# The end of an attention and soft-MoE kernel: where the last raw values and weights lie, a merge in halves, and outputs of two or three tiles a transfer

## The chip, the cores and the metric

The kernel runs on one core of a Trainium2 chip. The metric is the device time of one execution in microseconds (us). The core has five engines that run by themselves and meet at semaphores: TensorE (PE, its weight loads PEld), VectorE (DVE), ScalarE (ACT), GpSimd (POOL) and SyncE (SP). Sixteen DMA engines move data between HBM and SBUF. TensorE writes into PSUM. DMAs that cast float32 to bfloat16 are issued from POOL here, the plain ones from SP.

## The reference

```python
batch, n_heads, seq, head_dim = (8, 12, 448, 64)
N, D, E, S_per_e, F = (3584, 768, 8, 4, 1024)
# attention with one extra exp(-m) in the denominator
scores = scale * np.matmul(q, k.transpose(0, 1, 3, 2))
m = np.max(scores, axis=-1, keepdims=True)
e = np.exp(scores - m)
attn = e / (np.sum(e, axis=-1, keepdims=True) + np.exp(-m) + 1e-09)
attn_out = np.matmul(attn, v)
x = attn_out.transpose(0, 2, 1, 3).reshape(B * S, H * D)
# soft mixture of experts over all 3584 rows, 32 slots, 4 of them to an expert
logits = x @ phi
d = np.exp(logits - logits.max(0, keepdims=True)); d /= d.sum(0, keepdims=True) + 1e-09
slot_input = (d.T @ x).reshape(E, S_per_e, D)
for e in range(E):
    slot_out[e] = np.maximum(slot_input[e] @ w1[e], 0.0) @ w2[e]
c = np.exp(logits - logits.max(1, keepdims=True)); c /= c.sum(1, keepdims=True) + 1e-09
return c @ slot_out.reshape(n_slots, D)
```

## The kernel before

The attention runs over U = 24 units; a unit `u` is two heads of two batches (`bp, hp = divmod(u, 6)`). The rows of a batch are numbered `(p t)`: P = 64 partitions by TB = 7 tiles. For each unit, `stage_T` transposes q and k on TensorE, `stage_S` makes scores for the row maxima, `stage_MT` turns these into a mask operand (`md`, made by POOL at lines 282 and 288), `stage_ST` makes the scores once more with the maxima subtracted, ACT takes the exponential (line 309), `stage_AV` multiplies with v, and `stage_N` divides by the denominator into `xbuf(u)`. `stage_V` (line 314) casts the raw v. The last unit leaves the detour through SBUF out: `stage_last` (lines 380 to 400) divides straight from PSUM, with `last_sinks` having prepared the denominators. `stage_X` transposes x for the logits; `mixture` keeps a running softmax over rows for the 32 slots and adds the weighted rows to `acc`; `slot_in` is the matmul of it.

All instructions are issued in an order written by hand: `at(n, where, f)` puts a piece of work into the plan at tick `n` (7 ticks a unit, `end` is 168), and one loop over ticks runs the pieces in the order small, scores, av, value, ST, rooms, value, end, load. An engine carries out its own instructions in this order.

SBUF is laid out by hand. `block` holds the attention's buffers (`parts`); when their last reader is done, the same places take expert weights: `rooms[0..7]`, each 3072 bfloat16 columns, four quarters of 768 (`j0`, `m` of `load_w`). Room 1 covers the end of the raw v (`vr`) and the raw q and k (`qr`, `kr`). The first 24 weight pieces lie in `wres`; pieces 24 to 31 (`WRES` + 0..7) are the second matrices of experts 4 to 7 and go to the rooms. The weight loads are issued from POOL, the v loads from SP. v of unit 23 is loaded into the places `qr` and `kr`, after the transposes of unit 23 have read them; `stage_V(23)` then frees three quarters of room 1.

After the attention, `merge` finds weights for four partial sums of the slots (`rden`, `fw`, `sums`), `slot_in` ends in PSUM, line 674 adds it to `acc` into `ld`, line 678 transposes and folds it by 12 matmuls, and `den` (line 671) with `rden` (lines 682 and 683) gives the denominators; line 685 writes the experts' input `SI`. `experts_hidden` (line 705) does the first expert layer. `outer` (line 824) does the second one, into two PSUM halves of 384 columns; its last piece, `(1,)` of `jh` 1, needs rooms 4 to 7. Its results go to `so`; `first_tiles` makes the first two output tiles, and a loop makes tiles 2 to 27 (matmul line 884, copy 888, output DMA 889). PSUM tiles come from `ring`, three places taken in turn by `slot`. Output tile `i` is kept at its own place in `wres` (`kept`), 3072 bytes a partition, and tiles `t` of one `bp` lie side by side both there and in the output.

Of the kernel before, what the change touches and what calls it, by code (L numbers as in the profile page):

```python
# [9 lines left out]
F32 = mybir.dt.float32  # L10
# [14 lines left out]
def kernel(  # L25
# [75 lines left out]
    def xbuf(u):  # L101
        return block[:, ds(xbuf_at((u + 4) % (HP + 1)), N2)]

    def xruns(u):

        runs = []
        for i in range(HP):
            at_ = (u + i + 4) % (HP + 1)
            if runs and at_ > 1 and i % 4:
                runs[-1][1] += 1  # L110
            else:
                runs.append([i, 1, xbuf_at(at_)])
        return [(i, k, block[:, ds(o, k * N2)].rearrange("p (i s n) -> p i s n", i=k, s=TB))
                for i, k, o in runs]
# [40 lines left out]
        RAW[0, "qr"] = t_  # L155

    def load_v(u):
        t_ = block[:, ds(parts["vr" if u < U - 1 else "qr"][0], 2 * N2)].bitcast(F32).rearrange("p (h n) -> p h n", h=2)
        RAW[u, "vr"] = load(u, t_, v, nc.sync if u else nc.gpsimd)

    W = {}
# [5 lines left out]
    def load_w(i, j0=0, m=None, p0=0, rows=128):  # L167


        kind, e, half = weights[i]  # L170
        if kind == 1:
            J, n = KC // 2, F
            src = moe_w1[e].rearrange("(p j) f -> p j f", p=128)[:, ds(half * J, J), :]
        else:
            J, n = FK // 2, DD
            src = moe_w2[e, ds(half * 128 * J, 128 * J)].rearrange("(p j) f -> p j f", p=128)
        js = ds(2 * j0, 2 * (m or J))
        t_ = room(i, n // 2)
        src = src.rearrange("p j (h n) -> p (j h) n", h=2)
        gdma(out=t_[ds(p0, rows), js, :], in_=src[ds(p0, rows), js, :])  # L180
        for j in range(j0, j0 + (m or J)):
            W[kind, e, half * J + j] = t_[:, ds(2 * j, 2), :]
# [187 lines left out]

    def last_sinks(u):
        em = EM.pop(u)
        ems = small.tile([128, 2, TB], F32, tag="den", name="den").rearrange("p b g -> p (b g)")
        DEN[u] = ems
        for b in range(2):
            nc.gpsimd.tensor_copy(
                ems[:, ts(b, 2 * C3)].rearrange("p (h c) -> p h c", h=2), em[:, :, ds(b * C3, C3)])
        nc.gpsimd.tensor_copy(ems[:, ds(4 * C3, 2)], em[:, :, TB - 1])

    def stage_last(u):  # L380
        av = AV.pop(u)
        ems = DEN.pop(u)
        drec = small.tile([128, 2, TB], F32, tag="rec", name="rec", bufs=1).rearrange("p b g -> p (b g)")
        x = xbuf(u).rearrange("p (s n) -> p s n", s=TB)
        main = av[:, :, ds(0, 2 * C3 * 65)].rearrange("p b (g e) -> p b g e", e=65)
        rest = av[:, :, ds(2 * C3 * 65, 65)]
        nc.vector.scalar_tensor_tensor(
            drec[:, ds(0, 4 * C3)].rearrange("p (b g) -> p b g", b=2), main[:, :, :, D], 1e-9,
            ems[:, ds(0, 4 * C3)].rearrange("p (b g) -> p b g", b=2), op0=ALU.add, op1=ALU.add)
        nc.vector.scalar_tensor_tensor(drec[:, ds(4 * C3, 2)], rest[:, :, D], 1e-9,  # L390
                                       ems[:, ds(4 * C3, 2)], op0=ALU.add, op1=ALU.add)
        nc.vector.reciprocal(drec, drec)
        for b in range(2):
            nc.vector.tensor_tensor(
                x[:, ds(b * C3, C3), :].rearrange("p c (h d) -> p h c d", h=2),
                main[:, b].rearrange("p (h c) e -> p h c e", h=2)[:, :, :, ds(0, D)],
                drec[:, ts(b, 2 * C3)].rearrange("p (h c) -> p h c", h=2).unsqueeze(3)
                    .broadcast_to([128, 2, C3, D]), op=ALU.mult)
        nc.vector.tensor_tensor(
            x[:, TB - 1, :].rearrange("p (h d) -> p h d", h=2), rest[:, :, ds(0, D)],  # L400
            drec[:, ds(4 * C3, 2)].unsqueeze(2).broadcast_to([128, 2, D]), op=ALU.mult)
        X[u] = x


# [27 lines left out]
    def mixture(bp, n, at):  # L432
# [78 lines left out]

        def slot_in():

            ps = slot([128, DD])
            for s, (i, k, x) in ([(s, r) for r in xruns(bp * HP) for s in range(TB)] if final else
                                 [(s, r) for s in range(TB) for r in xruns(bp * HP)]):
                    b, c = divmod(s, C3) if s < 2 * C3 else (0, C3)
                    cs = ds(32 * c, 32)
                    nc.tensor.matmul(ps[cs, ds(i * 128, k * 128)], d_sb[:, b, cs], x[:, :, s, :],
                                     start=(b == 0 and i % 4 == 0), stop=(b == 1 or c == C3),  # L520
                                     tile_position=(0, 32 * c), skip_group_check=True)
            for i in range(HP):
                X.pop(bp * HP + i)
            if first:
                nc.vector.tensor_copy(acc, ps)
            elif not final:
                rescale(acc, alpha, ps)
            else:
                last_state["ps"] = ps

        if final:
            at(n - 28, "end", lambda: logits((0, 1)))
# [10 lines left out]
            at(n, "load", lambda: nc.gpsimd.memset(SI, 0.0))  # L543
            at(n + 5, "small", slot_sum)
            at(n + 7, "end", slot_in)
            at(n + 7, "end", lambda: [load_w(WRES + i) for i in (6, 7)])
            at(n + 7, "end", lambda: gate_logits(1))
            at(n + 7, "end", lambda: last_state["gl"][1]())
            at(n + 7, "end", experts_in)
# [200 lines left out]
    for u in range(U):  # L750
# [64 lines left out]

    os_ = [slot([128, 384]) for half in range(2)]

    def outer(half, jh, gs):
        J = FK // 2
        for g in gs:  # L820
            for j in range(J):
                for e in range(4):
                    es = ds(32 * e, 32)
                    nc.tensor.matmul(os_[half][es, :], HT[jh][:, g, j, es],
# [14 lines left out]
        return out[ds(2 * bp * S, 2 * S), :].rearrange("(q t) d -> q t d", t=TB)[:, ds(t, n), :]  # L839

    def kept(i, n=1):
        return wres[:, 2 + i // 2, ds(i % 2 * 2 * DD, 2 * DD * n)].bitcast(F32)

    def first_tiles(half, copy):


        ps = slot([128, 2, 512])
        for i in range(2):
            nc.tensor.matmul(ps[:, i, ds(0, 384)], wide[:, ts(i, 128)], so[:, half, :],
                             start=True, stop=True)  # L850
        o = kept(0, 2).rearrange("p (i g n) -> p i g n", i=2, g=2)[:, :, half, :]
        for i, n in ((0, 1), (1, 1)) if half == 0 else ((0, 2),):
            copy(o[:, ds(i, n)], ps[:, ds(i, n), ds(0, 384)])
            nc.sync.dma_start(out=rows_of(i, n)[:, :, ts(half, 384)], in_=o[:, ds(i, n)])

    outer(0, 0, range(G))
# [9 lines left out]
    nc.vector.tensor_copy(so[:, 1, :], os_[1])  # L866
# [53 lines left out]
```

## Time and profile before

| what | value |
|---|---|
| median of 3 runs | 322.11 us (321.18 to 323.55) |
| the profiled execution | 319.92 us, span 318.1 us |
| busy in the span: PE, DVE, POOL, ACT | 277.0, 253.6, 229.1, 211.7 us |
| DMA queue 0 (issued by POOL), queue 1 (by SP) | 36.46 MB, 22.03 MB |
| output transfers | 27 of 384 KB, 2 of 192 KB |
| last copy of an output tile ends | 304.56 us |

The span is the time from the first to the last instruction in the trace; the time of the execution also has what lies around it. The page cuts the span into 40 slices and gives the busy share of each engine in tenths. A group line names the line of the kernel, the engine, the operation and its tiles, the count, the busy time, the mean of one, and the idle time ahead with what ended it. Times inside the span are counted from its start.

### The profile page before, as it was taken

The page shows a single profiled execution, that of the slowest core. Times are in us where ns is not written, and L with a number is a line of the kernel's source. Part 1 is how long each engine was busy: PE and PEld are TensorE (multiplying, and loading weights), DVE is VectorE, ACT ScalarE, POOL GpSimd, SP SyncE. Part 2 cuts the span into 40 slices and gives each one's busy share as a digit, 9 for nine tenths or more (in the row PEclk, how much of TensorE's full clock was granted, in tenths as well). Part 3 has the DMA queues.
Part 4 walks back from the last instruction along what each step waited for, and adds up shares of the span by engine and source line. Part 5 has one row for each costly group of instructions (what it writes and reads, how often), then busy time and mean ns, then how long its engine had stood idle before and what let it go on. Part 6 is the DMA issues. An engine that isn't in the chain of part 4 may idle for free.

```text
span 318.1 us, 13342 instructions
## 1 busy us (share of the span) xinstructions
PE 277.0 (87%) x5861; PEld 159.1 (50%) x5862; DVE 253.6 (80%) x340; ACT 211.7 (67%) x338; POOL 229.1 (72%) x337
## 2 busy tenths in 40 slices
PE   1669989999899899999999999999999988986910
PEld 1325655465555465655655665555556545542300
DVE  2988988898799799999999999999999736527720
ACT  3026867777687677787877788777878885237610
POOL 7476798789898688899898889889984876620000
PEclk9999999999999999999999999999999999998555
DMA  7979999999999979999999999999999799958997
GB/s 131 172 94 187 178 169 190 172 169 183 184 184 192 158 118 174 176 182 145 195 170 184 149 155 202 179 153 154 181 184 195 123 156 202 214 119 305 396 400 287
DMA packets 49130, 59.34 MB, mean 187 GB/s; under 512 B 4560, under 2 KB 44496, under 8 KB 49072
## 3 DMA queue, kind: packets, MB, share of 16 engines
q0 software_dynamic: 37856, 36.46, 76.0%
q1 hardware_dynamic: 11216, 22.03, 20.9%
q8 instruction: 46, 0.75, 0.9%
q14 instruction: 12, 0.10, 0.1%
HBM read 83.46 MB, written 11.01 MB: 297 GB/s over the span
## 4 chain that ended last, share of the span: by engine, by line
PE 67%; DVE 11%; DMA 5%; POOL 5%; issue 4%; ACT 3%; SPq 0%; POOLq 0%; ACTq 0%; DVEq 0%
PE av L336 16%; PE ps L256 12%; PE ps L300 12%; PE ps L305 9%; PE ps L241 6%; DMA block<-in_moe_w_dram 4%; PE ps L419 3%; DVE block L264 3%; PE ps L884 3%; ACT block L309 2%; DVE m L264 2%; PE ps L260 2%; PE av L272 1%; POOL block L282 1%; DMA wres<-in_q_dram 1%
## 5 line engine op out<-in xcount | busy, mean ns | idle before, releaser
L309 ACT ACTIVATE block<-ps 128x896 bf16<-128x896 f32 x168 | 153.8, 917 | 56.0 <-PE ps L305 53.4
L264 DVE TENSOR_REDUCE block<-ps 128x2 bf16<-128x896 f32 x84 | 90.8, 1090 | 15.4 <-PE ps L256 13.8
L264 DVE TENSOR_REDUCE m<-ps 128x2 bf16<-128x896 f32 x84 | 90.8, 1090 | 4.7 <-PE ps L256 3.2
L336 PE MATMUL av<-block 64*128 64x65 bf16 (+1 forms) x2688 | 90.1, 193 | 3.1 <-issue 1.9
L336 PEld LDWEIGHTS <-block 64*128 64x128 bf16 (+1 forms) x2688 | 75.5, 97 | 32.5 <-issue 10.5
L300 PE MATMUL ps<-block,ones 64*64 64x448 bf16 x672 | 69.7, 368 | 4.5 <-POOL block L288 1.4
L305 PE MATMUL ps<-block 64*64 64x448 bf16 x672 | 66.4, 353 | 1.3 <-issue 1.3
L256 PE MATMUL ps<-block 64*128 64x448 bf16 x288 | 54.1, 372 | 3.3 <-DVE m L264 1.3
L256 PEld LDWEIGHTS <-block 64*128 64x128 bf16 x288 | 19.8, 94 | 52.6 <-issue 48.0
L282 POOL TENSOR_TENSOR block<-mt,nmask 128x768 bf16<-128x768 bf16 x24 | 35.2, 1468 | 12.7 <-ACT mt L276 11.6
L136 POOL DMA_DIRECT2D block<-in_q_dram x46 | 27.4, 602 | 18.7 <-PE ps L241 17.3
L364 POOL TENSOR_TENSOR block<-block,rec 128x896 bf16<-128x896 f32 x22 | 37.5, 1704 | 0.5
L180 POOL DMA_DIRECT2D wres<-in_moe_w_dram x48 | 35.0, 731 | 1.4
L300 PEld LDWEIGHTS <-ones 64*64 64x64 bf16 x672 | 24.7, 105 | 9.2 <-issue 4.1
L136 POOL DMA_DIRECT2D block<-in_k_dram x46 | 27.8, 622 | 1.2 <-ACT block L309 1.2
L244 DVE COPY block<-ps 128x896 bf16<-128x896 bf16 x48 | 27.8, 615 | 0.5 <-PE ps L241 0.3
L305 PEld LDWEIGHTS <-block 64*64 64x64 bf16 x672 | 24.5, 107 | 1.8 <-issue 1.7
L241 PE MATMUL ps<-ident,block 128*64 128x128 bf16 x644 | 24.6, 229 | 0.9 <-issue 0.4
L241 PEld LDWEIGHTS <-block 128*64 128x64 bf16 x644 | 20.4, 115 | 4.1 <-issue 2.0
L314 POOL CAST block<-block 128x896 bf16<-128x896 f32 x24 | 22.5, 937 | 0.0
L347 ACT COPY block<-av 128x780 f32<-128x780 f32 x22 | 17.7, 804 | 0.1
L420 DVE COPY block<-ps 128x896 bf16<-128x896 bf16 (+1 forms) x23 | 14.0, 607 | 1.8 <-PE ps L419 1.8
(161 smaller groups left out, 250.3 us busy)
## 6 DMA issues: line engine op xcount, KB each, us to landing
wres<-in_moe_w_dram POOLq DMA_DIRECT2D x48, 384.0 KB, 5.7
out_dram<-wres SPq DMA_DIRECT2D x27, 384.0 KB, 4.5
block<-in_v_dram SPq DMA_DIRECT2D x46, 224.0 KB, 6.2
block<-in_q_dram POOLq DMA_DIRECT2D x46, 112.0 KB, 6.2
block<-in_k_dram POOLq DMA_DIRECT2D x46, 112.0 KB, 6.2
block<-in_moe_w_dram POOLq DMA_DIRECT2D x4, 576.0 KB, 7.6
block<-in_moe_w_dram POOLq DMA_DIRECT2D x2, 768.0 KB, 11.4
block<-in_moe_w_dram POOLq DMA_DIRECT2D x6, 192.0 KB, 6.0
```

What stands on the lines that cost most here:

```text
L136: eng.dma_start(out=t_[ds(b * P, P), :, :], in_=src[bp * 2 + b, ds(hp * 2, 2)].rearrange("h (p t) d -> p h (t d)", t=TB))
L180: gdma(out=t_[ds(p0, rows), js, :], in_=src[ds(p0, rows), js, :])
L241: nc.tensor.transpose(ps[ds(h * D, D), :, ds(t * P, P)], r[:, h, ds(t * D, D)], ident)
L244: nc.vector.tensor_copy(t_, ps)
L256: nc.tensor.matmul(ps[:, h, ds(0, S)], QT[u][hs, b, ds(c * 128, 128)], KT[u][hs, b, :], start=True, stop=True)
L264: nc.vector.tensor_reduce(m[:, :, s], ps[:, :, ds(0, S)], axis=AX.X, op=ALU.max)
L282: nc.gpsimd.tensor_tensor(md[:, :, ds(0, C3 * 128)].rearrange("p b (e n) -> p b e n", n=P), mt.unsqueeze(1).unsqueeze(1).broadcast_to([128 ...
L300: nc.tensor.matmul(ps[ds(b * P, P), h, ds(0, S)], ones[hs, :], MD[u][hs, b, :], start=True, stop=False)
L305: nc.tensor.matmul(ps[ds(b * P, P), h, ds(0, S)], KT[u][hs, b, ds(t * P, P)], QT[u][hs, b, :], start=False, stop=True)
L309: nc.scalar.activation(et, ps[:, :, ds(0, S)], AF.Exp, scale=scale)
L336: nc.tensor.matmul(o, et[bs, h, ds(c * 128, w)], V65[u][bs, h, t, ds(0, 65)], start=(t == 0 and h == 0 and c == 0), stop=(t == TB - 1), sk ...
L364: (nc.gpsimd if u < U - 2 else nc.vector).tensor_tensor(x.rearrange("p s (h d) -> p h s d", h=2), xv[:, :, :, ds(0, D)], rec.unsqueeze(3). ...
```

## The change

The raw v of unit 23 is loaded into the places of `xbuf(22)` and `xbuf(23)`, whose earlier contents were read long before. Room 1 is then loaded in two halves, quarters 2 and 3 at tick 159 and quarters 0 and 1 at tick 163, where it was quarter 0 at tick 163 and quarters 1 to 3 at tick 166. The last weight piece (`WRES + 7`) is loaded as three quarters and one. `den` of unit 21 goes one tick later, behind the mask of unit 23.

The final `slot_in` writes two PSUM tiles of 384 columns, one for each three heads' pairs; `experts_in` adds and folds them one after the other, with the `den` product between them. For this a half of the contraction now holds 384 neighbouring rows of the first expert matrices, so their load takes neighbouring rows. The copy of `sums` goes from DVE to POOL, to the head of `merge`. `stage_last` handles its denominators as [2, 7] in one instruction instead of two.

`outer` of the last piece runs quarters 0 to 2 for both halves, then quarter 3 for both. `first_tiles(0)` uses a PSUM tile for each of its two output tiles. Tiles 2 and 3 of the first `bp` go out in one transfer, tiles 4, 5 and 6 by themselves; for every other `bp` tiles 0 and 1, 2 and 3, and 4 to 6 go out together.

```diff
-    def xruns(u):
+    def xruns(u, most=4):
...
-            if runs and at_ > 1 and i % 4:
+            if runs and at_ > 1 and i % most:
...
-        t_ = block[:, ds(parts["vr" if u < U - 1 else "qr"][0], 2 * N2)]...
+        t_ = block[:, ds(parts["vr"][0] if u < U - 1 else xbuf_at((U - 2 + 4) % (HP + 1)), 2 * N2)]...
...
-            src = moe_w1[e].rearrange("(p j) f -> p j f", p=128)[:, ds(half * J, J), :]
+            src = moe_w1[e, ds(half * 128 * J, 128 * J)].rearrange("(p j) f -> p j f", p=128)
...
-        nc.vector.scalar_tensor_tensor(
-            drec[:, ds(0, 4 * C3)].rearrange("p (b g) -> p b g", b=2), main[:, :, :, D], 1e-9,
-            ems[:, ds(0, 4 * C3)].rearrange("p (b g) -> p b g", b=2), op0=ALU.add, op1=ALU.add)
-        nc.vector.scalar_tensor_tensor(drec[:, ds(4 * C3, 2)], rest[:, :, D], 1e-9,
-                                       ems[:, ds(4 * C3, 2)], op0=ALU.add, op1=ALU.add)
+        nc.vector.scalar_tensor_tensor(drec, both[:, :, :, D], 1e-9, ems, op0=ALU.add, op1=ALU.add)
...
-            ps = slot([128, DD])
-            for s, (i, k, x) in ([(s, r) for r in xruns(bp * HP) for s in range(TB)] if final else
+            pss = [slot([128, DD // 2]) for _ in range(2)] if final else [slot([128, DD])]
+            for s, (i, k, x) in ([(s, r) for r in xruns(bp * HP, 3) for s in range(TB)] if final else
                                  [(s, r) for s in range(TB) for r in xruns(bp * HP)]):
+                    ps, i = (pss[i // 3], i % 3) if final else (pss[0], i)
...
-            at(n + 7, "end", lambda: [load_w(WRES + i) for i in (6, 7)])
+            at(n + 7, "end", lambda: [load_w(WRES + 6), load_w(WRES + 7, 0, 3), load_w(WRES + 7, 3, 1)])
...
     def merge():
+        nc.gpsimd.tensor_copy(sums, srun.broadcast_to([128, 128]))
...
-        nc.vector.tensor_copy(sums, srun.broadcast_to([128, 128]))
...
-        den = slot([128, NS])
-        nc.tensor.matmul(den, sums, rden, start=True, stop=True)
-        si = ld.rearrange("s (p j) -> s j p", j=KC)
+        si = ld.rearrange("s (a p j) -> s a j p", a=2, j=KC // 2)
         ps = spare(ds(0, KC * NS)).rearrange("p (j n) -> p j n", j=KC)
-        nc.vector.scalar_tensor_tensor(ld, acc, last_state["alpha"], last_state["ps"],
-                                       op0=ALU.mult, op1=ALU.add)
-        for j in range(KC):
-            for i in range(2):
-                nc.tensor.matmul(ps[:, j, :], si[:, j, :], fw[:, i, :], start=(i == 0), stop=(i == 1))
+        for a, half in enumerate(last_state["ps"]):
+            cs = ts(a, DD // 2)
+            nc.vector.scalar_tensor_tensor(ld[:, cs], acc[:, cs], last_state["alpha"], half,
+                                           op0=ALU.mult, op1=ALU.add)
+            for j in range(a * KC // 2, (a + 1) * KC // 2):
+                for i in range(2):
+                    nc.tensor.matmul(ps[:, j, :], si[:, a, j % (KC // 2), :], fw[:, i, :], start=(i == 0), stop=(i == 1))
+            if a == 0:
+                den = slot([128, NS])
+                nc.tensor.matmul(den, sums, rden, start=True, stop=True)
...
-            at(n + 20, "value", lambda u=u: stage_den(u))
+            at(n + (20 if u != U - 3 else 21), "value", lambda u=u: stage_den(u))
...
-    for n, i, js in ((end - 5, 0, (3, 1)), (end - 5, 1, (0, 1)), (end - 2, 1, (1, 3)), (end + 2, 2, (0, 2)),
+    for n, i, js in ((end - 9, 1, (2, 2)), (end - 5, 0, (3, 1)), (end - 5, 1, (0, 2)), (end + 2, 2, (0, 2)),
...
-    outer(0, 1, (1,))
+    for js in (range(3), (3,)):
+        for half in range(2):
+            outer(half, 1, (1,), js)
     nc.scalar.copy(so[:, 0, :], os_[0])
-    outer(1, 1, (1,))
     nc.vector.tensor_copy(so[:, 1, :], os_[1])
...
+    RUNS = {3: 2, 4: 1, 5: 1, 6: 1}, {1: 2, 3: 2, 6: 3}
...
-        nc.sync.dma_start(out=rows_of(i, 1)[:, 0, :], in_=o)
+        if t in RUNS[bp > 0]:
+            n = RUNS[bp > 0][t]
+            nc.sync.dma_start(out=rows_of(i - n + 1, n).rearrange("q t d -> q (t d)"), in_=kept(i - n + 1, n))
```

More of the change, by code (lines that the diff above doesn't have):

```diff
@@ L157, in load_v @@
     def load_v(u):
-        t_ = block[:, ds(parts["vr" if u < U - 1 else "qr"][0], 2 * N2)].bitcast(F32).rearrange("p (h n) -> p h n", h=2)
+        t_ = block[:, ds(parts["vr"][0] if u < U - 1 else xbuf_at((U - 2 + 4) % (HP + 1)), 2 * N2)].bitcast(F32).rearrange("p (h n) -> p h n", h=2)
         RAW[u, "vr"] = load(u, t_, v, nc.sync if u else nc.gpsimd)
@@ L372, in last_sinks @@
         em = EM.pop(u)
-        ems = small.tile([128, 2, TB], F32, tag="den", name="den").rearrange("p b g -> p (b g)")
+        ems = small.tile([128, 2, TB], F32, tag="den", name="den")
         DEN[u] = ems
@@ L376, in last_sinks @@
             nc.gpsimd.tensor_copy(
-                ems[:, ts(b, 2 * C3)].rearrange("p (h c) -> p h c", h=2), em[:, :, ds(b * C3, C3)])
-        nc.gpsimd.tensor_copy(ems[:, ds(4 * C3, 2)], em[:, :, TB - 1])
+                ems[:, b, ds(0, 2 * C3)].rearrange("p (h c) -> p h c", h=2), em[:, :, ds(b * C3, C3)])
+        nc.gpsimd.tensor_copy(ems[:, :, TB - 1], em[:, :, TB - 1])
     def stage_last(u):
@@ L382, in stage_last @@
         ems = DEN.pop(u)
-        drec = small.tile([128, 2, TB], F32, tag="rec", name="rec", bufs=1).rearrange("p b g -> p (b g)")
+        drec = small.tile([128, 2, TB], F32, tag="rec", name="rec", bufs=1)
         x = xbuf(u).rearrange("p (s n) -> p s n", s=TB)
-        main = av[:, :, ds(0, 2 * C3 * 65)].rearrange("p b (g e) -> p b g e", e=65)
-        rest = av[:, :, ds(2 * C3 * 65, 65)]
-        nc.vector.scalar_tensor_tensor(
-            drec[:, ds(0, 4 * C3)].rearrange("p (b g) -> p b g", b=2), main[:, :, :, D], 1e-9,
-            ems[:, ds(0, 4 * C3)].rearrange("p (b g) -> p b g", b=2), op0=ALU.add, op1=ALU.add)
-        nc.vector.scalar_tensor_tensor(drec[:, ds(4 * C3, 2)], rest[:, :, D], 1e-9,
-                                       ems[:, ds(4 * C3, 2)], op0=ALU.add, op1=ALU.add)
+        both = av[:, :, ds(0, TB * 65)].rearrange("p b (g e) -> p b g e", e=65)
+        nc.vector.scalar_tensor_tensor(drec, both[:, :, :, D], 1e-9, ems, op0=ALU.add, op1=ALU.add)
         nc.vector.reciprocal(drec, drec)
@@ L395, in stage_last @@
                 x[:, ds(b * C3, C3), :].rearrange("p c (h d) -> p h c d", h=2),
-                main[:, b].rearrange("p (h c) e -> p h c e", h=2)[:, :, :, ds(0, D)],
-                drec[:, ts(b, 2 * C3)].rearrange("p (h c) -> p h c", h=2).unsqueeze(3)
+                both[:, b, ds(0, 2 * C3)].rearrange("p (h c) e -> p h c e", h=2)[:, :, :, ds(0, D)],
+                drec[:, b, ds(0, 2 * C3)].rearrange("p (h c) -> p h c", h=2).unsqueeze(3)
                     .broadcast_to([128, 2, C3, D]), op=ALU.mult)
         nc.vector.tensor_tensor(
-            x[:, TB - 1, :].rearrange("p (h d) -> p h d", h=2), rest[:, :, ds(0, D)],
-            drec[:, ds(4 * C3, 2)].unsqueeze(2).broadcast_to([128, 2, D]), op=ALU.mult)
+            x[:, TB - 1, :].rearrange("p (h d) -> p h d", h=2), both[:, :, TB - 1, ds(0, D)],
+            drec[:, :, TB - 1].unsqueeze(2).broadcast_to([128, 2, D]), op=ALU.mult)
         X[u] = x
@@ L524, in slot_in @@
             if first:
-                nc.vector.tensor_copy(acc, ps)
+                nc.vector.tensor_copy(acc, pss[0])
             elif not final:
-                rescale(acc, alpha, ps)
+                rescale(acc, alpha, pss[0])
             else:
-                last_state["ps"] = ps
+                last_state["ps"] = pss
         if final:
@@ L816, with outer @@
     os_ = [slot([128, 384]) for half in range(2)]
-    def outer(half, jh, gs):
+    def outer(half, jh, gs, js=range(FK // 2)):
         J = FK // 2
         for g in gs:
-            for j in range(J):
+            for j in js:
                 for e in range(4):
@@ L841, in kept @@
     def kept(i, n=1):
-        return wres[:, 2 + i // 2, ds(i % 2 * 2 * DD, 2 * DD * n)].bitcast(F32)
+        return wres.rearrange("p a n -> p (a n)")[:, ds(2 * HW + i * 2 * DD, 2 * DD * n)].bitcast(F32)
     def first_tiles(half, copy):
[L847 to L850, printed above, removed]
         o = kept(0, 2).rearrange("p (i g n) -> p i g n", i=2, g=2)[:, :, half, :]
         for i, n in ((0, 1), (1, 1)) if half == 0 else ((0, 2),):
-            copy(o[:, ds(i, n)], ps[:, ds(i, n), ds(0, 384)])
+            ps = slot([128, n, 512])
+            for k in range(n):
+                nc.tensor.matmul(ps[:, k, ds(0, 384)], wide[:, ts(i + k, 128)], so[:, half, :],
+                                 start=True, stop=True)
+            copy(o[:, ds(i, n)], ps[:, :, ds(0, 384)])
             nc.sync.dma_start(out=rows_of(i, n)[:, :, ts(half, 384)], in_=o[:, ds(i, n)])
```

## The prediction

> **What bounds the kernel now.** I read the page first, for the shape of the span.
>
> ```profile
> PE 277.0 (87%) x5861; PEld 159.1 (50%) x5862; DVE 253.6 (80%) x340; ACT 211.7 (67%) x338; POOL 229.1 (72%) x337
> ...
> PE   1669989999899899999999999999999988986910
> ...
> PEclk9999999999999999999999999999999999998555
> DMA  7979999999999979999999999999999799958997
> GB/s 131 172 94 187 178 169 190 172 169 183 184 184 192 158 118 174 176 182 145 195 170 184 149 155 202 179 153 154 181 184 195 123 156 202 214 119 305 396 400 287
> ```
>
> One slice is 7.95 us. TensorE is full up to slice 35 (286 us); from there the DMA engines are full at 396 to 400 GB/s while TensorE fades out. The change touches only what lies behind 240 us, so the attention part is left as it is. Next the stretches of the tail:
>
> ```profile
> 294.00:304.00 10.00, 9.20 (x32) 2.64 (x29) 7.68 (x9) 6.79 (x9) 0.00 (x0) 0.50 1.02 396
> 304.00:314.00 10.00, 0.00 (x0) 0.00 (x0) 0.56 (x1) 0.00 (x0) 0.00 (x0) 0.50 1.02 399
> ```
>
> The last two columns are the DMA share and GB/s. The rate is the same while tiles are still made and after the last copy (304.56): the outputs are bound by the DMA engines, not by the tiles and not by the granted clock of 0.50. So the end is the moment when outputs start, plus the bytes at that rate. When they start is read in the chain of waits in order of time (start, duration, what):
>
> ```profile
> 270.97 0.55 POOL block L180
> 271.52 12.92 DMA block<-in_moe_w_dram
> 284.44 0.04 issue
> 284.48 1.47 PE ps L824 x29
> 285.95 0.02 issue
> 285.98 0.57 DVE wres L866
> ```
>
> The last expert weights (room 7) land at 284.44; TensorE waits for them, runs 29 matmuls in 1.47, and only then is `so` copied. The first output is issued at 286.91. Last, POOL's timeline ahead of it, since POOL issues the weights:
>
> ```profile
> 252.26 0.95 POOL L314 CAST block<-block 128x896 bf16<-128x896 f32 x1
> 253.51 0.53 POOL L180 DMA_DIRECT2D block<-in_moe_w_dram  x1 [0.30 <-POOL block L314]
> 254.05 0.23 POOL L356 TENSOR_TENSOR den<-block,em 128x14 f32<-128x14 f32 x1
> 254.23 1.47 POOL L282 TENSOR_TENSOR block<-mt,nmask 128x768 bf16<-128x768 bf16 x1
> 255.66 0.40 POOL L288 TENSOR_TENSOR block<-mt,nmask 128x128 bf16<-128x128 bf16 x1
> 256.02 1.68 POOL L364 TENSOR_TENSOR block<-block,rec 128x896 bf16<-128x896 f32 x1
> 257.65 0.58 POOL L180 DMA_DIRECT2D block<-in_moe_w_dram  x1
> ```
>
> Here the last pair's mask (L282, L288) waits behind a cast, a weight issue of room 1 and `den`.
>
> **The change, part by part: up to the weights.** The last raw v no longer goes to the q/k places, so three of room 1's four quarters need not wait for the cast of 252.26. Its 384 KB half (2,2) is issued as soon as the last transposes end (241.34), the other half at 251.7 with the issues there. POOL's 0.30 of idle, the issue of 0.53 and `den` (0.23) leave the stretch ahead of L282: 254.23 becomes 253.25, where DVE's `mt` of 252.98+0.23 allows no more. TensorE's idle time before the following L300 was only 0.35, so 0.35 is the gain there. Behind the moved `den` waits DVE's reciprocal of 254.32, now about 255.4; DVE then idles until 258.14, so that costs nothing, and L364 still starts by 255.7. The issue at 257.65 comes about 0.25 sooner.
>
> The early 384 KB run beside the last v loads: 128 rows of 3072 bytes over 16 engines, 8 rows of 248 ns (median of the packet records) = 2.0 us. The v halves land at 247.24 and 248.29; their casts start at 249.90 and 252.27. Pushed back by the full 2.0 they are still in time; without that cover each further us would be POOL's. On SP the v load loses its wait for the transposes, and nothing follows it until the outputs.
>
> What the queue gains: the 16 engines do not end together. Room 1's last piece ends at 258.2 to 259.3 on fifteen engines and at 260.03 on the last, by the landing records. That one starts the next room late and stays behind to the end: 282.7 to 283.8 for the others, 284.44 for it. With 2.0 us taken out before 258 it starts level: 0.7, and 0.25 from the earlier issue. Room 7 is now issued as 3+1 quarters: one more issue on POOL (0.55; behind it stand the clearing of `HT` and the subtraction at 273.45, which come 0.15 later under a DVE and ACT that wait for other things), and 8 x (361+135-474) ns = 0.18. So three quarters land at 284.44-0.95+0.18-8x0.135 = 282.6 and the last at 283.7. If the laggard gains nothing, 0.95 is 0, and they land at 283.5 and 284.6; I take the first, for the lag is there in every landing from 260 on.
>
> **The merge.** `stage_last` makes one sum of two: -0.1 (L387, L390). In halves, DVE merges 384 columns in half of 1.01, from 270.15 (the 0.22 copy of `sums`, 270.04, goes to POOL, idle until 270.20) to 271.25. But the four transposes of 270.26 to 270.92 stand ahead on TensorE, then 6 matmuls (0.37), the `den` product (0.31), 6 more: 272.0; the sum and reciprocal of `rden` (0.18+0.35) now follow `den` at 271.65 and end at 272.2, against 272.29 for today's product. Gain 0.1; bounds -0.2 to +0.5. TensorE thus reaches the last weights at 283.33-0.35-0.1-0.1 = 282.8.
>
> **Start of outputs.** From 282.8, 32 matmuls with three quarters there first take 1.47 + 0.15: half 0 ends near 284.4 (before 285.13), half 1 near 284.6 (before 285.95). The first tile needs one product, not two, before its copy (-0.2), and its second tile now waits for DVE's copy of `so` to free a place in the ring. First issue 286.0 instead of 286.91: -0.85 to be careful. Bounds: -0.6 (laggard gains nothing) to -1.15.
>
> **Outputs.** 29 transfers become 16; 7 of two tiles, 3 of three, each row then 6144 or 9216 bytes. No write row of that length is in the trace, so the price comes from these windows (294 to 314 and 288 to 289; count, MB, share of 16 engines):
>
> ```profile
> DMA packets 2924, 7.95 MB, mean 398 GB/s; under 512 B 335, under 2 KB 335, under 8 KB 2924
> ...
> q1 hardware_dynamic: 2924, 7.95, 101.8%
> ```
>
> ```profile
> DMA packets 235, 0.31 MB, mean 313 GB/s; under 512 B 31, under 2 KB 235, under 8 KB 235
> ...
> q1 hardware_dynamic: 235, 0.31, 90.4%
> ```
>
> 1.018 x 16 x 20 us, less 335 completions of some 8 ns, over 2589 rows of 3072 bytes is 125 ns (the records' median is 121); 0.904 x 16 over 204 rows of 1536 is 71 ns (median 66). So 55 ns are bytes per 1536 and 11 to 16 ns are paid per row. Rows of 6144: 231; of 9216: 341. Cast loads of 1536, 3072, 4608 and 6144 landed bytes make as straight a line: 135, 248, 361, 474 ns. Per engine 8 rows x (14 tiles x 5.5 + 9 tiles x 7.3) = 1.14 us by medians, 1.56 by means; I take 1.3. Bounds: nothing (rows cut up, or another limit) to the pace of the lagging engine (below), and a loss by the row of the rival. A fixed cost per row is also what the Trainium skill has ("DMA: Bandwidth & Descriptors", section "Why small descriptors are slow (HBM only)"): about 3 cycles per packet beside one for each 32 bytes. That would be 3 in 99 here, where the rows show 10 in 100, and by it the outputs would gain only 0.4 and the time be 320.9; no run here shows cycles.
>
> Waiting for a second tile: the third transfer keeps the engines busy until about 289.0, and tiles 2 and 3 are there at 288.2; tile 4 follows about 0.1 after the pair. Later tiles come every 0.59 (24 copies in 290.3 to 304.6) against 0.93 written. Loss 0.1.
>
> **Sum.** -0.85 -1.3 +0.1 = -2.05. The profiled execution took 319.92 (span 318.1), which is below all the runs shown (median 322.11); I take the difference from the median: 320.0.
>
> **Rivals.**
> No gain from long rows, because they are cut up or the memory sets the rate: 396 to 400 GB/s in every full stretch looks like a ceiling; against it, the lagging engine catches up, so single engines can go faster. Only the start is left: -0.85, 321.2. The same page of the Trainium skill (section "Specifications") puts one core's limit to HBM at about 358 GB/s; the trace writes 398, so I give it no more than this chance.
>
> More gain: fifteen engines land a transfer every 0.99 though 8 x 121 is 0.97, the one behind every 0.94 (299.11 to 317.03 over 19). If fewer, longer transfers let all go at that pace, 26 x 0.045 = 1.2 come on top: 322.11-3.25 = 318.9, and with the start at its bound of -1.15, 318.6: over 1% faster.
>
> Slower: long rows write worse. Packets of v, 1792 bytes on the same hardware queue, took 87 ns where others shared the engines, 149 per 3072. At that rate 23 merged tiles x 8 x 28 ns = 5.2 are lost; net +4.3, 326.4. It loses from 125.6 ns per 3072 on, where the start's 0.85 is eaten. For it: rows' times spread from 119 to 142. Against: the line from 1536 to 3072 points the other way.
>
> **How the numbers follow.** Forecast 0.55 (its own range 319.0 to 321.0), no gain from rows 0.18, more gain 0.15, slower 0.12. About 1% is what a measurement of this kernel can tell from no change: faster 0.15, same 0.73, slower 0.12. The range takes the first three, with the 1 us by which the runs shown differ: 317.9 to 323.0.
>
> **What would show it.** Right: the last mask at 253.3, the last weights by 283.8, first output issued at 286.0, about 425 GB/s in merged transfers with packets of 231 and 341 ns. Wrong: output packets still of 3072 bytes, or 398 GB/s with 16 transfers; casts of v that wait for DMA; room 7 landing at 284.4 or later.

## The result, and the profile after

The changed kernel takes 319.72 us in the median of 6 runs (317.12 to 322.27); the kernel before, run beside it, 322.71 (321.18 to 324.3, 6 runs). The ratio is 0.988, 95% interval 0.984 to 0.992; it leaves out slow runs, such as the one of 322.27, and the medians as they stand give 0.991. On a second chip session (label f2_after below) the medians were 318.45 to 322.34, ratio 0.988 (0.985 to 0.992). So the gain is some 3 to 4 us where 2.05 was forecast: inside the stated range, but the sum lacked a term.

The one profiled execution of each hides this: 320.44 (span 318.7) after, 319.92 (span 318.1) before. The profile before lies below the six runs of its kernel and the one after above its median. One stretch makes the difference: from the first exponential of unit 12 to that of unit 22 the trace before takes 102.3 us and the one after 104.8, the least and the most of all fourteen traces. So stretches are compared here, not spans, and over all traces that the experiments left. First the chain of waits of the changed kernel, in order of time (start, duration, what):

```profile
271.96 0.55 POOL block L180
272.52 12.67 DMA block<-in_moe_w_dram
285.19 0.04 issue
285.23 1.31 PE ps L823 x25
286.55 0.02 issue
286.57 0.49 ACT wres L865
287.06 0.04 issue
287.10 0.34 PE ps L850
287.43 0.02 issue
287.46 0.49 ACT wres L852
```

The weights still end the wait. But TensorE now waits for three quarters of room 7 (285.19); the last quarter lands at 286.14, while it works. Both halves of `so` now end close together: ACT copies the first at 286.57, DVE the second 0.16 later, where it was 0.65 before. One product (0.34) stands ahead of the first tile's copy. POOL's timeline ahead of it:

```profile
253.84 0.95 POOL L314 CAST block<-block 128x896 bf16<-128x896 f32 x1
254.90 1.46 POOL L282 TENSOR_TENSOR block<-mt,nmask 128x768 bf16<-128x768 bf16 x1
256.33 0.39 POOL L288 TENSOR_TENSOR block<-mt,nmask 128x128 bf16<-128x128 bf16 x1
256.69 0.21 POOL L356 TENSOR_TENSOR den<-block,em 128x14 f32<-128x14 f32 x1
257.25 1.69 POOL L364 TENSOR_TENSOR block<-block,rec 128x896 bf16<-128x896 f32 x1 [0.35 <-DVE rec L362]
258.88 0.58 POOL L180 DMA_DIRECT2D block<-in_moe_w_dram  x1
```

The mask follows the cast at once, `den` stands behind it, and L364 waits 0.35 for DVE's reciprocal, which the prediction did not have. The outputs in stretches (the last two columns are DMA share and GB/s):

```profile
294.00:304.00 10.00, 9.75 (x36) 2.95 (x33) 8.05 (x9) 6.51 (x9) 0.00 (x0) 0.52 1.02 411
304.00:314.00 10.00, 0.33 (x2) 0.00 (x0) 1.07 (x2) 0.68 (x1) 0.00 (x0) 0.50 1.02 420
```

411 and 420 GB/s, where before had 396 and 399, at the same DMA share.

### The profile page after: what moved, and what is told of

The parts are those of the page before. It is cut to its first block, busy times and chain, and to the rows that moved or that the text cites. A ratio compares the mean times of both kernels' runs of the same rounds, so it can differ in the third digit from the quotient of the medians.

```text
span 318.7 us, 13327 instructions
## 1 busy us (share of the span) xinstructions
PE 277.5 (87%) x5862; PEld 159.4 (50%) x5862; DVE 253.5 (80%) x339; ACT 211.7 (66%) x338; POOL 230.2 (72%) x339
## 4 chain that ended last, share of the span: by engine, by line
PE 71%; DVE 11%; DMA 5%; issue 3%; ACT 3%; POOL 1%; SPq 0%; ACTq 0%; DVEq 0%; POOLq 0%
PE av L336 17%; PE ps L256 13%; PE ps L300 12%; PE ps L305 9%; PE ps L241 6%; DVE block L264 4%; DMA block<-in_moe_w_dram 4%; PE ps L885 3%; PE ps L414 3%; DVE m L264 2%; PE ps L260 2%; ACT block L309 2%; PE av L272 1%; DMA wres<-in_q_dram 1%; PE ps L451 1%
## 5 line engine op out<-in xcount | busy, mean ns | idle before, releaser
L364 POOL TENSOR_TENSOR block<-block,rec 128x896 bf16<-128x896 f32 x22 | 37.5, 1706 | 0.8 <-DVE rec L362 0.4
```

The costliest lines, as they stand in the source:

```text
L364: (nc.gpsimd if u < U - 2 else nc.vector).tensor_tensor(x.rearrange("p s (h d) -> p h s d", h=2), xv[:, :, :, ds(0, D)], rec.unsqueeze(3). ...
```

## The experiments

Four times are read from every trace. A: first exponential of unit 0 to first of unit 12. B: first exponential of unit 22 to the issue of the first output. C: that issue to the last landing; C8: to the last transfer's landing on the 8th of the 16 engines, from the landing records (a transfer counts 16 landings, one an engine). The ratio is to the kernel before, run in the same session, with its 95% interval. Each trace is one execution, and among traces of like kernels A and B scatter by 1 to 2 us, so means over several traces are compared; a single trace settles little.

| run | what it has of the change | A | B | C | C8 | ratio |
|---|---|---|---|---|---|---|
| before | nothing | 124.9 | 38.4 | 30.1 | 29.3 | 1 |
| e1_outputs | outputs | 124.8 | 39.3 | 29.5 | 28.4 | 0.995 (0.992 to 0.999) |
| e2_weights | weights | 125.1 | 37.9 | 30.9 | 29.3 | 0.994 (0.991 to 0.998) |
| h1_rooms | first part of weights | 124.5 | 39.2 | 30.2 | 29.8 | 1.000 (0.996 to 1.003) |
| h2_last | second part of weights | 125.8 | 38.3 | 30.2 | 29.3 | 0.996 (0.993 to 1.000) |
| e3_merge | merge, w1 | 123.0 | 39.0 | 30.1 | 29.4 | 0.991 (0.988 to 0.995) |
| e4_w1 | w1 | 124.4 | 39.1 | 30.3 | 29.4 | 0.993 (0.989 to 0.996) |
| after | all | 123.9 | 37.9 | 29.8 | 28.3 | 0.988 (0.984 to 0.992) |
| f2_after | all | 123.1 | 38.3 | 29.6 | 28.3 | 0.988 (0.985 to 0.992) |
| f1_single | all but outputs | 122.8 | 37.9 | 30.0 | 29.3 | 0.990 (0.987 to 0.993) |
| o2_rows | all, rows of 3072 | 122.7 | 38.6 | 30.5 | 29.2 | 0.990 (0.985 to 0.994) |
| w2_apart | all, w2 rows apart | 123.5 | 37.4 | 29.8 | 28.3 | 0.990 (0.984 to 0.995) |
| g1_spare | all, one transfer cut | 123.6 | 38.4 | 31.5 | 30.2 | 0.996 (0.993 to 1.000) |
| g2_spare2 | the same and a load cut | 122.3 | 38.3 | 31.3 | 30.5 | 1.000 (0.996 to 1.003) |

**One part at a time.** The first four runs add one part each to the kernel before. Their ratios together take off some 0.02 (0.005, 0.006, 0.009) where the whole change takes off 0.012; with some 0.004 of doubt on each, the ratios don't divide the gain, and the stretches have to.

e1_outputs:

```diff
...
-        nc.sync.dma_start(out=rows_of(i, 1)[:, 0, :], in_=o)
+        if t in RUNS[bp > 0]:
+            n = RUNS[bp > 0][t]
+            nc.sync.dma_start(out=rows_of(i - n + 1, n).rearrange("q t d -> q (t d)"), in_=kept(i - n + 1, n))
...
```

> Before with the outputs of two and three tiles alone. Theory A (rows cost 11 to 16 ns less often, every engine gains): 1.3 us faster, ratio 0.996. Theory B (the end is set by the one engine that lost about 1 us to a fetch of instructions at 293.4, and this one was not held by its rows): fifteen engines land pairs 1.9 us apart instead of 1.98, the one behind gains about 0.026 us a tile, 0.5 us in all, ratio 0.998. Rival C (rows longer than 3072 bytes gain nothing): ratio 1.000.

C falls to 29.5, C8 to 28.4 (mean of the seven traces with single tiles, f1_single among them: 30.24 and 29.38; of the four with merged rows and nothing cut: 29.69 and 28.33). The two sets don't overlap. Both theories hold, each for its engines: the 8th engine gains 1.05 us, the engine that ends last 0.55, and the last one makes the time. So theory B is right on the end; the ratio, 0.995, can't tell the two apart.

The merged outputs gain a little more behind the last landing: from there to the end of the span it is 1.09 us in every trace with 29 transfers and 0.91 in every one with 16. SP ends with a row of waits for semaphores of 0.06 us each, and four of them stood behind the last landing, now one.

e2_weights, in words:

```diff
+ the moved v, (end - 9, 1, (2, 2)) and (end - 5, 1, (0, 2)), the later den
+ load_w(WRES + 7, 0, 3), load_w(WRES + 7, 3, 1), outer in two steps, two PSUM tiles in first_tiles
```

> Before with the moved v, room 1 in two halves, the later den, room 7 in three quarters and one, the order of the last outer products and two PSUM tiles for the first outputs; merge and outputs as before. Prediction's theory: first output 0.85 us sooner after the last exponential (23.5 us in both traces so far), ratio 0.997. Rival: the sixteen engines are full from the first load of room 2 on, which is issued behind the mask as before, so the start of the outputs does not move: ratio 1.000, first output still 23.5 us behind the last exponential.

B is 37.9, against a mean of 38.95 (38.4 to 39.3) in the four traces with neither half of the weight part. Over the seven traces with the whole part and no load cut it is 37.4 to 38.6, mean 38.04. The prediction's theory holds for the size, which rests on these means and not on this one trace; the measure that the expectation used, from the last exponential, was a poor one, as the earlier mask moves the exponentials too.

e3_merge and e4_w1:

```diff
...
-            src = moe_w1[e].rearrange("(p j) f -> p j f", p=128)[:, ds(half * J, J), :]
+            src = moe_w1[e, ds(half * 128 * J, 128 * J)].rearrange("(p j) f -> p j f", p=128)
...
-        si = ld.rearrange("s (p j) -> s j p", j=KC)
+        si = ld.rearrange("s (a p j) -> s a j p", a=2, j=KC // 2)
...
```

> Before with the merge in halves, the copy of sums on POOL, one sum in stage_last and the neighbouring rows of w1; weights and outputs as before. Theory: the path from slot_in to the experts' first matmul gains 0.1 us or nothing and is covered by the wait for the weights: ratio 1.000. Rival: the neighbouring rows of w1 make the weight loads quicker and the attention's waits shorter: 1 to 2 us, ratio 0.994 to 0.997.

> Before with the neighbouring rows of w1 alone (the fold reads its columns in the matching order). If the attention is bound by TensorE the loads hide as before: ratio 1.000, and half of the exponentials done at 146 us. Rival: loads of neighbouring rows land sooner and the gain beyond the tail comes from here: ratio 0.994 to 0.997.

The rival holds in both. w1's neighbouring rows alone give 0.993, and e3_merge, which has them too, 0.991. A is 124.5 to 125.8 in the five traces with w1's rows apart and 122.3 to 124.4 in the nine with neighbouring rows: means 125.03 and 123.25, 1.8 us. The two sets do not overlap, if only just: e4_w1's own trace has the 124.4, and it is the fourteen traces together with the ratios of e3_merge and e4_w1 that show the gain. The two DMA views below are of before and of e4_w1, from 21 to 146 us (count, MB, share of 16 engines):

```profile
q0 software_dynamic: 17294, 15.72, 85.4%
```

```profile
q0 software_dynamic: 17303, 15.73, 82.9%
```

The same bytes take 2.5% of 125 us less on each engine, 3.1 us. Over all traces the share is 85.4 to 86.2% for 15.7 MB with rows apart, and 82.5 to 85.3% for 15.7 to 16.1 MB with neighbouring ones; the 85.3 is the changed kernel's own. By the packet records of all 12288 packets of w1 (1024 landed bytes) the mean took 113.2 to 115.1 ns with rows apart and 106.5 to 111.5 with neighbouring ones, at one median of 98; packets over 1.5 times the median were 5.8 to 6.6% and 4.2 to 5.0%. What TensorE gains by it is seen in its waits from 21 to 146 us, those of no visible releaser ("issue"; us in total, times, longest; rows of TensorE alone), before, in e4_w1 and in f1_single, which has the least of all traces:

```profile
PE av L336 <- issue: 1.7, 3, 0.9
PE ps L305 <- issue: 1.3, 1, 1.3
PE ps L300 <- issue: 1.1, 1, 1.1
PE av L272 <- issue: 0.5, 1, 0.5
PE ps L241 <- issue: 0.4, 1, 0.4
```

```profile
PE av L336 <- issue: 2.7, 2, 2.3
...
PE ps L300 <- issue: 0.7, 1, 0.7
...
PE ps L305 <- issue: 0.5, 1, 0.5
```

```profile
PE ps L300 <- issue: 1.1, 1, 1.1
```

Over all traces such waits over 0.15 us in stretch A sum to 4.0 to 5.0 us with rows apart (mean 4.4) and 1.1 to 3.9 with neighbouring ones (mean 2.8). All waits of TensorE there, with those that have a visible releaser, have means of 5.5 and 4.1: 1.4 of the 1.8.

What they wait for can be read from the records. Queue 8 fetches instructions, 16 KB at a time, on the same DMA engines; there are 46 fetches for some 11780 matmuls and weight loads of TensorE, one for every 256. In the attention the fourteen traces have 113 such waits. Every one ends 1.2 to 1.7 us behind the end of a fetch, though fetches come only some 6 us apart, and they fall on the same few places of TensorE's program, multiples of 256 records apart to within one. So these are waits for instructions. With rows apart the fetches also start later: TensorE then has on average 145 to 147 records to go to the place where the next 256 begin, and 148 to 160 with neighbouring rows, and again the sets do not overlap, if narrowly. That the slower weight packets are what delays the fetches fits this, but no run changed the fetches alone.

**Both ways and the lagging engine.** The next four ran in one session.

> The changed kernel once more, to stand beside the others on one chip: ratio 0.986 to 0.991, first output 23.5 us behind the last exponential, first output to last landing 29.5 to 29.8 us; where the waits of TensorE for instructions in the attention fall differs from run to run.

As expected for the ratio and for C; B is 38.3.

f1_single takes the merged outputs back (the diff of e1_outputs reversed):

> The changed kernel with one output tile a transfer, as before (29 transfers). Theory B (one engine lags behind a fetch of 16 KB of instructions and sets the end; longer rows give it 0.5 us): first output to last landing 30.1 to 30.8 us, as in the four other traces with single tiles, against 29.5 to 29.8 with merged ones; ratio to before 0.990. Theory A (1.3 us for every engine): ratio 0.992. Rival (the whole gain of the change is in the outputs): ratio 1.000.

C is 30.0, C8 29.3, as in the other traces with single tiles. The ratio is 0.990 against 0.988 of the whole: the rival falls, as most of the gain is there without the merged outputs. The ratio can't tell theory B from theory A; C and C8 do.

g1_spare (the first piece below) and g2_spare2 (both pieces):

```diff
-            nc.sync.dma_start(out=rows_of(...)..., in_=kept(i - n + 1, n))
+            for q0, q in ((0, 120), (120, 8)) if i in (24,) else ((0, 128),):
+                nc.sync.dma_start(out=rows_of(...)...[ds(q0, q)], in_=kept(i - n + 1, n)[ds(q0, q)])
...
-    (end + 7, 3, (1, 2)),
+    (end + 7, 3, (1, 2, 0, 120)), (end + 7, 3, (1, 2, 120, 8)),
```

> The changed kernel, with the last transfer of two tiles (tiles 2 and 3 of the last bp) cut into 120 partitions and 8. If the engine that lags is the one that serves the last 8 of 128 partitions, its lag of 1.5 us at the end (317.77 against 316.26 for the median engine) goes and the end is set by the others, 0.25 later for their extra row: 1.2 us sooner than the changed kernel, ratio to it 0.996, first output to last landing 28.5 us. If another engine lags, or if the engines share one limit, the last landing stays 1 to 1.5 us behind the median engine and the time is the same or 0.3 longer.

> As the run before, and also one weight load of 384 KB (room 3, quarters 1 and 2) cut into 120 partitions and 8. If the same engine makes the last weights late (285.19 against 283.3 for the median engine), three quarters of room 7 land within 0.5 us of the median engine, TensorE starts the last products about 1 us sooner (284.2, where its own work ends), and the first output comes 22.5 us behind the last exponential instead of 23.5; 1 us more, ratio to the changed kernel 0.993. Rival: the weights' landing is held by all engines alike, and nothing moves.

Both were misses, and for a reason that none of their theories had. The 120 partitions did go to 15 engines: one of the 16 counts comes at 304.7 us, at the issue, the others from 314.7 on. But the engines then finish apart: the last transfer lands between 316.9 and 319.6 us, where in the changed kernel fourteen engines land within 0.2 us (316.2 to 316.4) and the other two at 317.0 and 317.8. C grows by 1.8. The packets themselves slow down while the cut transfers are written: from 311 to 316 us rows of 6144 bytes took 362 ns in the mean, up to 1287, where they took 239 in the 7 us before that; g2_spare2 shows the same (352 from 309 to 314). Why is left open. In g2_spare2 three quarters of room 7 land 1.5 us behind the 8th engine (283.1 against 281.6; 1.9 in the changed kernel, 285.2 against 283.3), and B is 38.3 as in f2_after, so the start did not move, as the rival had it. Which engine lags is left open by these two.

**What of the weights, what of the rows.** The last four.

h1_rooms and h2_last split e2_weights in two, the first and second line of its diff:

> Before with the moved v, room 1 in two halves at ticks 159 and 163 and the later den alone. The four traces without the change's weight part need 38.4 to 39.3 us from the first exponential of unit 22 to the first output, the five with it 37.9 to 38.4; unit 22 to unit 23 is 8.32 us in the former and 7.78 in the latter. If the mask's earlier start is the gain: 7.78 here, and 0.5 us less to the first output (38.4), ratio 0.998. If the lagging DMA engine also gains by the earlier weights: 0.9 us less, 38.0, ratio 0.997.

> Before with room 7 in three quarters and one, the order of the last outer products and two PSUM tiles for the first outputs alone. Unit 22 to 23 as before (8.32). If the products behind the last quarter are the gain: 0.4 us less from the first exponential of unit 22 to the first output (38.5 against a mean of 38.95), ratio 0.999. Rival: the extra load and its rows cost what the order gains: 38.95, ratio 1.000.

h2_last: B is 38.3, 0.7 less than the mean and at the edge of the four traces without the part (38.4 to 39.3); it points to its theory's gain, but one trace does not show it. h1_rooms: unit 22 to 23 takes 7.78 us, as expected, yet B is 39.2. Room 2's load is issued 8.80 us behind unit 22's first exponential instead of 9.19, but room 7 lands 27.92 behind that issue. This last interval is 26.8 to 27.9 (mean 27.4) in the five traces with room 7 loaded in one, and 26.8 to 27.9 (mean 27.3, to the last quarter) in the eight with it in two and no load cut. It scatters more than the 0.4 to be found, so h1_rooms doesn't tell whether its gain lasts; nor does it give a sign that the lagging engine gained.

o2_rows:

```diff
-        return wres.rearrange("p a n -> p (a n)")[:, ds(2 * HW + i * 2 * DD, 2 * DD * n)].bitcast(F32)
+        w = 2 * DD + 16
+        return wres.rearrange("p a n -> p (a n)")[:, ds(2 * HW + i * w, w * n)].bitcast(F32).rearrange(
+            "p (i n) -> p i n", i=n)[:, :, ds(0, DD)]
```

> The changed kernel with the same 16 output transfers, but the tiles kept 32 bytes apart in SBUF, so that every row written is 3072 bytes long again. If it is the length of rows that quickens the outputs: fifteen engines 0.99 us a tile as with single tiles, the lagging one 0.945, first output to last landing 30.2 us, and 0.6 us slower than the changed kernel. If it is the number of transfers (fewer issues and completions): 0.95 us a tile and 29.6 as with the change.

The DMA views of o2_rows (294 to 312 us) and of the changed kernel (296 to 314 us):

```profile
DMA packets 2472, 7.18 MB, mean 399 GB/s; under 512 B 134, under 2 KB 134, under 8 KB 2472
...
q1 hardware_dynamic: 2472, 7.18, 102.5%
```

```profile
DMA packets 1235, 7.54 MB, mean 419 GB/s; under 512 B 145, under 2 KB 145, under 8 KB 936
...
q1 hardware_dynamic: 1235, 7.54, 101.8%
```

Twice the packets at 399 GB/s, against 419 with long rows, with the same 16 transfers. The 8th engine takes 0.989 us a tile and the last one 0.939, as with single tiles (0.990 to 0.994 and 0.939 to 0.943), and C is 30.5. So it is the length of the rows that sets the pace, not the number of transfers. The ratio, 0.990, can't tell.

w2_apart, in which w2's rows meet hidden columns that are not theirs, tries the finding of w1 on w2:

```diff
+            src = moe_w2[e].rearrange("(p j) f -> p j f", p=128)[:, ds(half * J, J), :] if i < WRES else ...
```

> The changed kernel with the first eight pieces of w2 (loaded in the second half of the attention) taken 12 KB of every 24 KB, as w1 was before the change, instead of neighbouring rows; its hidden columns then meet other rows of w2, so it computes something else. If rows taken apart slow the loads and with them the attention: packets of 768 landed bytes over 1.5 times their median grow from the changed kernel's share, as those of w1 do (6.1 to 6.9% against 4.3 to 5.2%), and the second half of the attention (exponential 84 to the end of the last) takes 0.8 us more than the 119.0 us of the traces with neighbouring rows; ratio to before 0.991 instead of 0.988. Rival: the gain of w1's rows in the first half was chance: no change there, ratio 0.988.

Half a miss. The packets of 768 bytes behave as expected: mean 91.3 ns and 5.3% over 1.5 times the median, against 86.3 to 89.8 and 3.7 to 4.6% in all other traces. But the second half of the attention takes 117.8 us, no more than in the others (117.3 to 119.3). That is what the rival foretold, so this run does not bear out the finding of w1; against chance there stand the two ratios and the fourteen values of A above. Two things differ here. The slowing is smaller, some 3 ns a packet over 8192 packets where w1 had some 6 over 12288. And fetches of instructions start with 184 to 198 records to go, in this trace 184, the fewest, instead of 145 to 160, so a later one costs less; TensorE's waits of no visible releaser are 1.4 us in this trace and 0.2 to 2.8 in the others. That slower packets cost time only where something waits for the DMA engines is the reading that fits both, not one that is shown.

## Why the prediction was right or wrong

**The missing term.** The prediction dismissed the attention: "The change touches only what lies behind 240 us, so the attention part is left as it is." The diff has one line that acts before that, the rows of w1, and it had no term in the sum. It is the largest: 1.8 us in stretch A, and 0.7% of the time (0.4 to 1.1) in the run that has it alone. The page before had a sign that the DMA engines matter in the attention: queue 0 alone took 76% of sixteen engines, and most of their slices there are at 9. That w1 also folds faster is small: the 12 products of line 678 took 0.73 us before and 0.49 in e4_w1:

```profile
272.14 0.49 PE L678 MATMUL av<-fw,ld 128*128 128x32 bf16 x12 [0.40 <-DVE ld L674]
```

**The start of the outputs: 0.85 forecast, 0.9 measured** (B 38.95 to 38.04). Its terms: "The issue at 257.65 comes about 0.25 sooner" is 0.39 (9.19 to 8.80 behind unit 22). The mask's 0.35 is 0.54 (unit 22 to 23, 8.32 to 7.78 in every trace with the part): TensorE lost more than the 0.35 that was read as its wait, perhaps because what it did meanwhile came back later. "one product, not two" is 0.19 (1.58 to 1.39 from the first copy of `so` to the issue). Half 0 is copied 0.42 behind the landing instead of 0.89. But "starts level: 0.7" failed: room 7 lands no sooner behind room 2's issue, 27.4 and 27.3. Counted from unit 22's first exponential in the trace before (248.47), the last quarter lands at 284.6 in the mean, not at 283.7; "room 7 landing at 284.4 or later" was the prediction's own sign of being wrong. The engine does start more level: its lag behind the 8th engine on room 2's first load is 0.2 to 0.5 us in six of the nine traces with the moved v, and 0.8 to 2.4 in the five without. So the lag that stays to the end is not the one from room 1. In the changed kernel's landing records it is 0.4 on room 2's first load (263.4 against 263.0 for the 8th engine) and 2.2 on the next (266.4 against 264.2). It is made anew there. Fetches of instructions start at 259.5 and 265.7 and take 1.1 and 0.9 us of an engine. They can be part of the cause, but the lag grew by 1.8 us, and a second engine fell behind by 1.1 there too; the rest is open.

**The outputs: 1.3 forecast, 0.55 measured.** The price of a row was near: medians of 236 and 351 ns for 6144 and 9216 bytes, forecast 231 and 341. But the gain is a small difference: a tile's share of such a row is 118 and 117 ns against 121, which saves 3 and 4 ns and not 5.5 and 7.3, or by the means some 6 and 7 (125 to 119 and 118). The 8th engine gains 1.05, below the 1.3 and within what these two would give (0.6 and 1.2). The step that failed is "Per engine 8 rows x (14 tiles x 5.5 + 9 tiles x 7.3)", taken for all engines alike. The one that lands last is 2 us behind the 8th from 295 us on, across another fetch (293.4 before, 294.6 after), still 0.8 behind at the end before and 1.5 after, and it was running at 0.943 us a tile while the others were held to 0.991. With long rows the others go to 0.943, it to 0.918. The rule of the Trainium skill that the prediction weighed ("DMA: Bandwidth & Descriptors", section "Why small descriptors are slow (HBM only)") gave 0.4: too little for the 8th engine, nearer than the rows' price for the one that ends. The rival of more gain had seen these two paces, and the others did reach the faster one; but the engine at that pace sets the end, and it had less to win. The rival without gain from rows falls with 419 GB/s; the same page's 358 GB/s a core (section "Specifications") is not what the trace shows.

**Merge and the rest.** From the end of the last exponential to the experts' first product 9.19 became 8.95, and 8.94 with w1 alone: the halves by themselves gave nothing, where 0.1 was forecast. TensorE's two waits there, 0.40 for line 674 and 0.18 for the experts' input, became one of 0.62 for the experts' input. The later reciprocal of DVE, said to cost nothing, made POOL wait 0.35 ahead of L364; room 2's issue stands behind L364, so it could have come that much sooner still. What this would have been worth at the outputs no run shows.

The sum as it was: 1.8 + 0.9 + 0.55, and 0.2 behind the last landing, is some 3.4, between the 3.0 of the medians and the 3.9 of the ratio. The stretch from unit 12 to unit 22 that lies between A and B adds nothing clear: 103.5 us in the mean with rows apart, 103.9 with neighbouring ones. That the median of 319.72 lies so near the forecast 320.0 is luck: start and outputs gave 1.5 where 2.05 was summed, less than forecast, and a term that was put at nothing gave 1.8. The forecast of within 1% was too little by the ratio, 1.2% (0.8 to 1.6); over 1% was given 0.15, and not for this mechanism.

## What to carry to other kernels

Give every line of a diff a term, layouts of loads too, even where the engine that waits seems not to wait for them. When a stage is bound by DMA engines, ask which of the sixteen ends it: a gain that all have in the records reaches the time only as far as the last one has it. And set a sum of 2 us against stretches of many traces: the kernel before alone ran from 321.18 to 324.3 us in six executions.

## What the runs showed of the hardware

Weight loads of the same bytes and the same rows of 12 KB a partition took 3.1 us an engine less over 125 us (82.9% against 85.4%, e4_w1 and before) when the partitions' rows lay side by side in HBM than when their starts lay 24 KB apart; the median packet was the same, 98 ns, and 4.2 to 5.0% of the packets, not 5.8 to 6.6%, took over 1.5 times that.

TensorE's instructions came in 46 fetches of 16 KB, each 0.9 to 1.9 us of a DMA engine in the attention. All 113 waits of TensorE in the attention that were over 0.15 us and had no visible releaser, in fourteen traces, ended 1.2 to 1.7 us behind the end of such a fetch.

The DMA engine that lands last falls 1.5 to 2.7 us behind the 8th in the outputs of every trace across a 16 KB fetch, where it was 0.4 to 0.9 behind on the transfer ahead. It catches up by 0.05 us a tile with single tiles and 0.025 with merged ones. A second engine falls 0.4 to 1.0 behind there. On the last weight load its lag is 1.2 to 2.3 us in every trace but g2_spare2 (0.4). The Trainium skill ("DMA: Bandwidth & Descriptors", section "Latency and other measured facts") has two engines usually slower, and guesses at the descriptor rings of DMAs issued from GpSimd. Here the lag also grows among outputs issued from SP, 0.9 behind the 8th engine on the pair of tiles 2 and 3 and 2.2 on the next tile (294.44 and 296.65 against 293.5 and 294.5). The runs don't tell which engine it is. A transfer of 120 partitions used 15 engines, but while it and its rest of 8 partitions were written, rows took 362 ns in the mean instead of 239, and on the last transfer the engines ended 2.7 us apart.
